# A block's normed, transposed tokens kept in DRAM between two uses; one pool of weight tiles; a new written-out order

## The chip, the cores and the metric

The kernel runs on one core of a Trainium2 chip. TensorE (PE) multiplies matrices, VectorE (DVE) and ScalarE (ACT) work on tiles in SBUF and PSUM, GpSimd (POOL) does a few small operations and issues transfers, and SyncE (SP) only issues transfers. Sixteen DMA engines move the data. The metric is the device time of one execution in microseconds (us), as a median over runs; less is better.

## The reference

Input are 2048 tokens of 512 elements (bf16), eight memory tokens, and the weights of one attention layer (32 heads of 128) and of one gated FFN (512 to 1792 and back). Both layers are applied twice, with the same weights:

```python
x = x + A(layernorm(x), mem0, Wq, Wk, Wv, Wo, 32)
x = x + B(layernorm(x), w_gate, w_up, w_down)
x = x + A(layernorm(x), mem0, Wq, Wk, Wv, Wo, 32)
x = x + B(layernorm(x), w_gate, w_up, w_down)

def A(x, mem0, Wq, Wk, Wv, Wo, seg):      # recurrent over 64 segments of 32 tokens
    mem = mem0
    for s in range(64):
        h = concat(mem, x[32*s : 32*s+32])          # 8 + 32 = 40 tokens
        q, k, v = h @ Wq, h @ Wk, h @ Wv            # per head
        p = softmax(mask(q @ k.T / sqrt(128)))      # memory seen by all, the rest causal
        o = (p @ v) @ Wo
        mem = o[:8]; out[s] = o[8:]
    return concat(out)

def B(x, w_gate, w_up, w_down):
    return (sigmoid(x @ w_gate) * (x @ w_up)) @ w_down
```

The memory makes the segments a chain: a segment's eight memory tokens come from the one before.

## The kernel before

**Steps.** The two passes (job 0 and job 1) run at the same time, job 1 six segments behind job 0 (`lag=6`). Step t handles segment t of job 0 and segment t - 6 of job 1, so there are 70 steps; steps 0 to 5 hold job 0 alone, steps 64 to 69 job 1 alone. A step (`emit_step`, L771 and on) has, for six heads at a time: Q and K projections (L868), scores (L904), mask, maximum, exponential and sum on DVE and ACT, a transpose of the probabilities (L950), the product with V (L976) and the output projection (L995), whose first rows become the next step's memory. The tokens of a step lie transposed in one of eight tiles `hT`.

**Blocks.** Four segments make a block of 128 tokens, sixteen blocks per job. After the last step of a block its FFN runs (`ffn`): transposes back (L1065), residual, LayerNorm, gate and up products (L1097), tanh form of the sigmoid, the down product (L1120). In job 0 the result is normed again and becomes job 1's tokens.

**V.** Most rows of V do not depend on the memory, so V is computed for whole blocks ahead of the steps (`v_pass`, L635, with 128 columns of tokens at a time), written to a DRAM scratch `scr` and read back into `vsb` by the steps. The remaining rows are computed in each step (`strips`, L762). For job 0, ten blocks (2, 14, 3, 4, 5, 7, 8, 10, 11, 13) get their V in `v_group` while the weights are loaded; for 6, 9, 12, 15 and the rest of 14 `v_fill` norms the block and its V rows are done eight at a time, beside job 1's V of some block. Blocks 0 and 1 are taken from `pre1`.

**LayerNorm.** `layernorm_T` (L575 to L596) does statistics on DVE (L582 to L584), a power of -1/2 on POOL (L585), the scaling on DVE into one of two tiles `xn` (L586), and four 128x128 transposes on PE (L595) into a PSUM bank. It is called through `ln_x` for the V of job 0, and again for the same block in `pre1`, which loads the block's tokens into one of six tiles `xs` (L739), norms and transposes them, and copies them into the four `hT` tiles of its segments (`write_hT_x`, L605).

**Weights.** Wq, Wk, Wv, Wo (16.8 MB) stay in SBUF, loaded at the start by SP (L511), each piece of Wv after the piece two before it. The FFN weights do not fit: each block streams them anew, seven pieces each of gate, up and down (256 KB a piece), by POOL (L1089, L1090, L1114) into rings `wg`, `wu`, `wd` of three tiles each. While the weights load at the start these nine tiles serve as staging for V (`bootp`), and every V write of that time carries the key "boot", on which the first loads into the rings wait.

**What sets the order.** All work is first collected as tasks with keys that are read and written. A planner holds an order found elsewhere, stored as a compressed string (`SEQUENCE`), and a bit for each task that may run on either of two engines. `replay` walks through it, gives out buffers of the pools (a free one, or the one freed longest ago), and adds the waits. Instructions are emitted in that order, so each engine and each DMA queue works through its part strictly in sequence. Two further rules: a large weight transfer on POOL waits for a matmul near its planned start (`pace`), and where the plan has PE idle for some time, `warm` puts dummy matmuls on a tile of zeros (L1214). The eight PSUM banks are one pool in which the kinds "bg" and "v" may each hold three at most.

## Time and profile before

| | |
|---|---|
| median of 3 runs (lowest to highest) | 1747.63 us (1746.31 to 1748.25) |
| span of the profiled execution | 1747.1 us; the page gives no other time of it |
| TensorE clock granted, mean | 1.000 |
| PE busy | 1733.4 us |
| DVE, ACT, POOL busy | 1248.4, 1128.5, 859.0 us |
| DMA | 273.41 MB, mean 156 GB/s |

How to read the lines below. PE is a matmul, PEld a weight load into the array, POOLq and SPq the issuing of transfers. The lines of stages give for a stretch its length, the busy time and number of instructions of each engine in the order PE, PEld, DVE, ACT, POOL, then the clock granted to TensorE, the mean busy share of the DMA engines (as transfers overlap it can pass 1) and GB/s. The chain is followed back from the last instruction, at each step to what released it. A group's line has the line number, engine, operation, output and inputs with shapes, the number of instructions; then busy time, the mean duration of one in ns, and the idle time before them with what ended it. Matmuls overlap in the array, so a matmul's duration is longer than the distance from one to the next. L numbers are those of the kernel before.

### The profile page before, as it was taken

What the parts mean: (1) busy time and instruction counts of PE and PEld (TensorE: products, weight loads), DVE (VectorE), ACT (ScalarE), POOL (GpSimd) and SP (SyncE); (2) the same over time, 40 slices, a digit from 0 to 9 for tenths busy, and PEclk for the clock granted to TensorE, in tenths of its full rate; (3) what the DMA queues carried; (4) which work ended last, traced back from release to release, by engine and by line L of the source; (5) the groups of instructions that cost most, each with busy time, mean ns of one, the idle gap of its engine ahead of it and who ended that gap; (6) DMA issues with size and microseconds to landing.
All of it is one profiled execution on the core that took longest, in us unless ns stands there. A gap on an engine that the chain in (4) does not pass through costs nothing.

```text
span 1747.1 us, 91842 instructions
## 1 busy us (share of the span) xinstructions
PE 1733.4 (99%) x39162; PEld 1491.8 (85%) x39162; DVE 1248.4 (71%) x4208; ACT 1128.5 (65%) x3119; POOL 859.0 (49%) x1367
## 2 busy tenths in 40 slices
PE   9999999999999999999999999999999999999998
PEld 4688789889898988989888888989888888988886
DVE  5677777677767776786777767776777776767676
ACT  3576777566666766666666666666665666666564
POOL 5624345635544554445445554544455364454543
PEclk9999999999999999999999999999999999999999
DMA  8935355645645555545555464545455464554644
GB/s 285 320 100 155 109 151 161 195 113 153 174 130 163 156 159 143 165 125 164 152 148 158 136 184 128 166 138 153 132 174 166 139 174 128 144 156 131 178 120 134
DMA packets 145583, 273.41 MB, mean 156 GB/s; under 512 B 39686, under 2 KB 86018, under 8 KB 145174
## 3 DMA queue, kind: packets, MB, share of 16 engines
q0 software_dynamic: 72944, 198.79, 39.8%
q1 hardware_dynamic: 72230, 68.75, 13.3%
q8 instruction: 307, 5.03, 1.2%
q14 instruction: 102, 0.84, 0.2%
HBM read 221.78 MB, written 27.07 MB: 142 GB/s over the span
## 4 chain that ended last, share of the span: by engine, by line
PE 94%; DMA 3%; DVE 1%; SPq 1%; issue 1%; POOL 0%; ACT 0%; POOLq 0%; ACTq 0%
PE bank L868 34%; PE bank L995 17%; PE bank L1097 12%; PE bank L762 8%; PE bank L635 6%; PE bank L1120 6%; PE bank L904 4%; PE bank L976 4%; PE bank L950 2%; PE bank L595 1%; PE bank L1214 1%; DMA wk_sb<-in_A_Wk_dram 1%; DMA wo_sb<-in_A_Wo_dram 0%; PE bank L1065 0%; DMA scr<-wu 0%
## 5 line engine op out<-in xcount | busy, mean ns | idle before, releaser
L868 PE MATMUL bank<-hT,wq_sb 128*128 128x80 bf16 (+3 forms) x8960 | 616.4, 198 | 1.0 <-DVE hT L1008 0.3
L868 PE MATMUL bank<-hT,wk_sb 128*128 128x80 bf16 (+3 forms) x8960 | 616.3, 198 | 0.8 <-DMA wk_sb<-in_A_Wk_dram 0.6
L1228 ACT CAST qku<-bank 128x480 bf16<-128x480 f32 (+4 forms) x770 | 384.7, 508 | 223.7 <-PE bank L868 194.6
L868 PEld LDWEIGHTS <-wq_sb 128*128 128x128 bf16 x8960 | 454.2, 99 | 32.1 <-issue 15.1
L868 PEld LDWEIGHTS <-wk_sb 128*128 128x128 bf16 x8960 | 446.9, 99 | 1.1 <-DMA wk_sb<-in_A_Wk_dram 0.7
L995 PE MATMUL bank<-otsb,wo_sb 128*128 128x80 bf16 (+1 forms) x8960 | 360.2, 198 | 2.2 <-DMA wo_sb<-in_A_Wo_dram 1.3
L918 DVE TENSOR_TENSOR st<-bank,cst 40x240 f32<-40x240 f32 (+3 forms) x768 | 280.5, 368 | 113.2 <-PE bank L904 97.5
L995 PEld LDWEIGHTS <-wo_sb 128*128 128x128 bf16 x8960 | 336.6, 99 | 15.5 <-DMA wo_sb<-in_A_Wo_dram 2.0
L1228 ACT CAST otsb<-bank 128x480 bf16<-128x480 f32 (+3 forms) x420 | 200.2, 483 | 83.4 <-PE bank L976 52.8
L1090 POOL DMA_DIRECT2D wu<-in_B_w_up_dram x217 | 166.5, 768 | 170.0 <-PE bank L950 36.4
L1114 POOL DMA_DIRECT2D wd<-in_B_w_down_dram x217 | 156.9, 723 | 182.0 <-PE bank L1120 39.6
L1224 POOL DMA_DIRECT2D vsb<-sst x351 | 178.2, 512 | 129.6 <-ACT sst L1228 64.7
L1089 POOL DMA_DIRECT2D wg<-in_B_w_gate_dram x217 | 166.4, 767 | 138.1 <-PE bank L1097 56.7
L928 ACT ACTIVATE st<-st 80x240 f32<-80x240 f32 (+3 forms) x420 | 159.2, 381 | 58.0 <-DVE st L925 54.8
L1097 PE MATMUL bank<-xnT,wg 128*128 128x128 bf16 (+2 forms) x1784 | 171.5, 218 | 0.0
L1097 PE MATMUL bank<-xnT,wu 128*128 128x128 bf16 (+2 forms) x1784 | 171.1, 218 | 0.0
L930 DVE TENSOR_REDUCE small<-st 80x6 f32<-80x240 f32 (+3 forms) x420 | 151.5, 363 | 23.4 <-ACT st L928 20.2
L1220 ACT ACTIVATE ptsb<-bank,small 120x160 bf16<-120x160 bf16 (+3 forms) x430 | 156.6, 386 | 17.2 <-PE bank L950 10.7
L904 PE MATMUL bank<-qku 128*128 128x80 bf16 (+1 forms) x2240 | 162.7, 197 | 1.0 <-issue 0.9
L925 DVE TENSOR_TENSOR st<-st,small 80x240 f32<-80x240 f32 (+3 forms) x420 | 155.0, 370 | 5.7
L939 DVE TENSOR_TENSOR pb<-st,small 80x240 bf16<-80x240 f32 (+3 forms) x420 | 154.1, 370 | 5.7
L923 DVE TENSOR_REDUCE small<-st 80x6 f32<-80x240 f32 (+3 forms) x420 | 152.5, 364 | 6.2
(108 smaller groups left out, 2554.1 us busy)
## 6 DMA issues: line engine op xcount, KB each, us to landing
wg<-in_B_w_gate_dram POOLq DMA_DIRECT2D x220, 256.0 KB, 4.2
wu<-in_B_w_up_dram POOLq DMA_DIRECT2D x220, 256.0 KB, 4.2
wd<-in_B_w_down_dram POOLq DMA_DIRECT2D x220, 256.0 KB, 3.9
vsb<-scr SPq DMA_DIRECT2D x137, 66.0 KB
scr<-vst SPq DMA_DIRECT2D x90, 96.0 KB
vsb<-scr POOLq DMA_DIRECT2D x93, 66.0 KB, 3.4
vsb<-sst SPq DMA_DIRECT2D x179, 32.0 KB
vsb<-sst POOLq DMA_DIRECT2D x169, 32.0 KB, 2.8
```

The source lines that it names most:

```text
L868: nc.tensor.matmul(o_ap, lhsT=W[:, c, h * P:(h + 1) * P], rhs=mv(c), start=(c == 0), stop=(c == DC - 1))
L904: nc.tensor.matmul(s_all(SB)[:, w0 + i, :], lhsT=fview(qku[:, i, 0, 0:1], [(1, P)]), rhs=qku[:, i, 1, 0:ncol], start=True, stop=True)
L918: pl.add("DVE", dve_ns(n, True), lambda gsz=gsz, hs=hs, st=st, SB=SB, pj_=pj_, npj_=npj_, mk=mk, idx=idx: nc.vector.tensor_tensor(out=st[p ...
L928: pl.add("ACT", act_ns(n), lambda hs=hs, st=st: nc.scalar.activation(out=st[pr, hs], in_=st[pr, hs], func=ACTF.Exp, scale=self.scale), r=s ...
L995: nc.tensor.matmul(WB[:, c * ncol:(c + 1) * ncol], lhsT=self.wo[:, h, c * P:(c + 1) * P], rhs=otsb[:, hl, 0:ncol], start=(h == 0 and c == ...
L1089: pl.add("POOL", 760, lambda wg=wg, fs=fs: nc.gpsimd.dma_start(out=wg[:], in_=self.wgv[:, :, fs]), r=[("wo", self.H - 1)], w=[gk] + bt, la ...
L1090: pl.add("POOL", 760, lambda wu=wu, fs=fs: nc.gpsimd.dma_start(out=wu[:], in_=self.wuv[:, :, fs]), r=[("wo", self.H - 1)], w=[uk] + bt, la ...
L1097: nc.tensor.matmul(gu[:, 2 * i + k, 0:n], lhsT=W[:, c, i * P:(i + 1) * P], rhs=xnT[:, c, rw], start=(c == 0), stop=(c == DC - 1))
L1114: pl.add("POOL", 760, lambda wd=wd, ip=ip: nc.gpsimd.dma_start(out=wd[:], in_=self.wdv[:, 2 * ip:2 * ip + 2, :]), w=[dk] + (["boot"] if se ...
L1220: nc.scalar.activation(out=dst, in_=src, func=ACTF.Copy, scale=by)
L1224: {"SP": nc.sync, "POOL": nc.gpsimd}[tk.on].dma_start(out=got[1], in_=got[2])
L1228: nc.scalar.copy(out=dst, in_=src)
```

## The change

1. `ln_x` norms and transposes a block once. The result is copied from PSUM into a tile of `vst`, and written to a DRAM tensor `xt` (128 KB per block). The block is noted as kept.
2. A later `ln_x` or `pre1` of a kept block calls `kept_x`: it reads the block from `xt` into one of the two tiles `xn` by SP, and the copies into `hT` are made from there. `pre1` still loads the block's tokens into `xs`, which the residual needs.
3. The three rings of three tiles become one pool `wtp` of nine tiles. A load takes a tile from it, whichever of gate, up and down it is for. V's staging at the start draws on the same pool, and the key "boot" is gone.
4. The pool of PSUM banks has no caps by kind.
5. `SEQUENCE` is a new order, for the new list of tasks.

```diff
+        self.xt = dr.tile([self.NBLK * P, D], BF16, name="xt")
...
-        self.NG, self.ND = 3, 3
-        self.wg = [c.tile([P, DC, 2 * P], BF16, name=f"wg{i}") for i in range(self.NG)]
-        self.wu = [c.tile([P, DC, 2 * P], BF16, name=f"wu{i}") for i in range(self.NG)]
-        self.wd = [c.tile([P, 2, D], BF16, name=f"wd{i}") for i in range(self.ND)]
+        self.wt = [c.tile([P, 1024], BF16, name=f"wt{i}") for i in range(9)]
...
-        self.bank = Pool([...], {"bg": 3, "v": 3}, psum=True)
+        self.bank = Pool([...], psum=True)
...
-        self.bootp = Pool([fview(w[:, 0, 0:1], [(1, 1024)]) for w in self.wd + self.wg + self.wu])
+        self.wtp = Pool(self.wt)
...
     def ln_x(self, b, boot=True):
+        if b in self.kept:
+            return self.kept_x(b)
...
-        return self.layernorm_T(xb[:, :], key)
+        pst, B = self.layernorm_T(xb[:, :], key)
+        nc, pl, D = self.nc, self.pl, self.D
+        tt = pl.buf(self.vstp)
+        pl.add(("ACT", "DVE"), copy_ns(D, True), lambda: (tt[:, 0:D].rearrange("p (c n) -> p c n", c=self.DC), pst()), r=[B], w=[tt])
+        pl.add(("SP", "POOL"), {"SP": 430, "POOL": 590}, lambda: ("dma", self.xt[b * P:(b + 1) * P, :], tt[:, 0:D]), r=[tt], w=[("xt", b)], lat=3000.0, nb=P * D * 2)
+        self.kept.add(b)
+        return pst, B
+
+    def kept_x(self, b):
+        nc, pl, D = self.nc, self.pl, self.D
+        tt = pl.buf(self.xnp)
+        pl.add("SP", 430, lambda: nc.sync.dma_start(out=tt[:, :], in_=self.xt[b * P:(b + 1) * P, :]), r=[("xt", b)], w=[tt], lat=3500.0, nb=P * D * 2)
+        return (lambda: tt[:, :].rearrange("p (c n) -> p c n", c=self.DC)), tt
...
-        pst, B = self.layernorm_T(xb[:], ("xs", i))
+        pst, B = self.kept_x(b) if b in self.kept else self.layernorm_T(xb[:], ("xs", i))
...
+    def weight(self, wt, nm, jp, keys, after):
+        nc = self.nc
+        src = self.wdv[:, 2 * jp:2 * jp + 2, :] if nm == "wd" else (self.wgv if nm == "wg" else self.wuv)[:, :, jp * 2 * P:(jp + 1) * 2 * P]
+        n = 2 if nm == "wd" else self.DC
+        self.pl.add("POOL", 760, lambda: nc.gpsimd.dma_start(out=wt[:, 0:1024].rearrange("p (c f) -> p c f", c=n), in_=src), w=keys, lat=4700.0, nb=370000, r=after)
...
-                gi = self.nxt("wg", self.NG)
-                wg, wu, gk, uk = self.wg[gi], self.wu[gi], ("wg", gi), ("wu", gi)
...
+                wg, wu = gk, uk = pl.buf(self.wtp), pl.buf(self.wtp)
+                for wt, nm in ((wg, "wg"), (wu, "wu")):
+                    self.weight(wt, nm, jp, [wt], [("wo", self.H - 1)])
...
-                di = self.nxt("wd", self.ND)
...
+                wd = dk = pl.buf(self.wtp)
+                self.weight(wd, "wd", ip, [wd], [("wo", self.H - 1)])
```

In the changed kernel the lines move: transposes of LayerNorm are L587, V passes L627, strips L769, Q and K L875, scores L911, output projection L1002, gate and up L1104, down L1125, dummies L1219.

## The prediction

> **What bounds the kernel now.** I read the page first, then busy time by stage, the chain that ended last, and the groups of instructions. From the page:

> ```profile
> span 1747.1 us, 91842 instructions
> PE 1733.4 (99%) x39162; PEld 1491.8 (85%) x39162; DVE 1248.4 (71%) x4208; ACT 1128.5 (65%) x3119; POOL 859.0 (49%) x1367
> ```

> TensorE is idle for 13.7 us of 1747.1. By stage (length, busy time per engine, granted clock, DMA share, GB/s):

> ```profile
> 0.00:10.23 10.23, 9.17 (x36) 3.72 (x37) 4.22 (x13) 1.76 (x2) 3.65 (x19) 1.00 0.70 214
> 10.23:43.68 33.45, 31.09 (x201) 14.41 (x202) 19.64 (x54) 13.75 (x30) 20.85 (x43) 1.00 0.92 306
> 43.68:79.00 35.32, 33.23 (x576) 21.20 (x572) 21.43 (x67) 18.81 (x58) 21.74 (x43) 1.00 1.01 343
> 131.00:1700.00 1569.00, 1566.06 (x35729) 1375.30 (x35727) 1136.13 (x3836) 1032.20 (x2807) 774.45 (x1203) 1.00 0.53 151
> 1700.00:1747.10 47.10, 41.88 (x1089) 33.61 (x1085) 30.39 (x106) 22.33 (x79) 19.12 (x28) 1.00 0.47 134
> ```

> There are two regimes. From 131 to 1700 us TensorE is idle for 2.94 us of 1569, and the DMA engines are half used: only fewer matmuls, or fewer of those few waits, shorten it. The first 79 us look as busy, but from 10 us on the DMA share is 0.92 and then 1.01. The chain says which of the two decides there (start, us, what):

> ```profile
> 18.17 7.47 DMA wv_sb<-in_A_Wv_dram
> 32.51 5.86 DMA wq_sb<-in_A_Wq_dram
> 38.38 7.48 DMA scr<-wu
> 51.15 10.87 DMA wk_sb<-in_A_Wk_dram
> 69.99 8.54 DMA wo_sb<-in_A_Wo_dram
> 78.58 0.84 PE bank L995 x20
> 79.75 2.51 PE bank L868 x96
> ```

> Step 0 ends with matmuls on `wo` (L995) that wait for the last piece of Wo, landed at 78.5 us; step 1 starts at 79.75. Until then the V passes of ten blocks fill TensorE. The load is bound by bytes, the rest by the stream of matmuls.

> **1. Fifteen LayerNorms go.** Before, a block is normed once for V (ten in `v_group`, five in `v_fill`) and all sixteen again in `pre1`: 31. After, blocks 0 and 1 are normed in `pre1` and 2 to 15 once, for V: 16. The written-out order agrees: 60 transposes on L595 fewer. What one takes:

> ```profile
> 12.83 0.61 PE L595 MATMUL bank<-cst,xn 128*128 128x128 bf16 x8
> L595 PE MATMUL bank<-cst,xn 128*128 128x128 bf16 x312 | 29.7, 219 | 0.1
> ```

> Eight take 0.61 us, 0.219 of it the last one's own length: (0.61 - 0.219) / 7 = 56 ns from one to the next, and sixty are 3.4 us. They lie in the stream after the load, where nothing hides a matmul: **-3.4 us**, the one certain term. The other engines' parts, and the nearest rows for the new copy:

> ```profile
> L582 DVE BATCH_NORM_STATS2 small<-xs 128x6 f32<-128x512 bf16 x36 | 24.7, 685 | 5.1 <-DMA xs<-in_A_x_dram 4.8
> L586 DVE TENSOR_SCALAR xn<-xs,small 128x512 bf16<-128x512 bf16 x36 | 15.1, 421 | 4.4 <-POOL small L585 4.1
> L585 POOL TENSOR_TENSOR small<-small,cst 128x1 f32<-128x1 f32 x78 | 46.2, 593 | 154.8 <-DVE small L584 148.4 <-DVE hT L1230 6.1
> L1228 ACT COPY xvf<-bank 128x384 bf16<-128x384 bf16 x4 | 1.9, 474 | 9.5 <-PE bank L595 9.5
> L1228 ACT CAST sst<-bank 128x512 bf16<-128x512 f32 x98 | 57.1, 589 | 63.8 <-PE bank L762 56.1 <-DVE xn L586 3.5 <-PE bank L673 1.5
> ```

> VectorE loses at least 15 x (0.685 + 0.421) = 16.6 us, GpSimd 15 x 0.593 = 8.9. Fourteen copies of 512 elements out of PSUM are new, 0.474 to 0.589 us each, some 7.5 us over two engines that are busy 71% and 65%. I count neither: both hide under TensorE. Where that cover is gone a late copy costs its 0.6 us.

> **2. Fourteen writes of `xt`, fifteen reads, one x load fewer.** Each moves 131 KB. In the body they are 3 MB at a DMA share of 0.53: hidden. In the load they are not. In plan order 24.5 MB stand ahead of the last weight, 23.45 before: V's scratch writes ahead of it are the same 4.89 MB, eight `xt` writes are new (three on SP, five on POOL). At 343 GB/s, the rate of the full stage, their 1.05 MB put the last piece of Wo 3.1 us later. Two things pay back. One more V group, four matmuls on L635, stands before step 1:

> ```profile
> 10.23 2.76 PE L635 MATMUL bank<-wv_sb,xvf 128*128 128x512 bf16 x12
> L635 PE MATMUL bank<-wv_sb,xvf 128*128 128x512 bf16 x224 | 53.2, 379 | 2.4 <-DMA wv_sb<-in_A_Wv_dram 2.4
> ```

> That is 4 x (2.76 - 0.379) / 11 = 0.9 us that later steps need not do. And the stage from 10.23 to 43.68 has 8% of its DMA time free, 2.7 us. With none of it used the load costs 3.1 - 0.9 = +2.2, with all of it -0.5. The chain runs through DMA and the SP queue in that stage too, so its free time is mostly a queue waiting for a copy; I credit 0.8 us of it: **+1.4 us**. [...]

> **3. Queues.** SP goes from 1098 transfers to 1060, GpSimd from 1255 to 1321: 49 loads of V from scratch move from SP to GpSimd, which also takes seven `xt` writes.

> ```profile
> L1224 POOL DMA_DIRECT2D vsb<-scr x176 | 94.8, 540 | 62.3 <-PE bank L976 27.7 <-DMA scr<-vst 14.7 <-PE bank L950 12.1
> L1089 POOL DMA_DIRECT2D wg<-in_B_w_gate_dram x217 | 166.4, 767 | 138.1 <-PE bank L1097 56.7 <-PE bank L995 17.2 <-PE bank L904 13.3
> DMA to landing us min/median/max: 3.2/4.2/6.3
> PE bank L976 <- DMA wg<-in_B_w_gate_dram: 0.2, 1, 0.2
> ```

> 66 x 0.54 - 8.9 = 27 us more on an engine busy for 859 of 1747: covered, unless a weight load stands behind it (below). A read of `xt` waits on SP for one of two `xn` tiles; what stands behind it are V loads and scratch writes, of which more than before go by GpSimd. It then keeps the tile until four copies into `hT` are done, so an FFN's LayerNorm may find one tile only. I count 0; at most five such meetings of one GpSimd step, 5 x 0.593 = 3 us.

> **4. One pool of nine weight tiles, new order, no caps on PSUM kinds.** No instruction is added. Adding up the matmuls in the two orders, step 12 begins after 289 us of work in both, step 57 after 1,443 and 1,440: the removed transposes and no larger move. The new order can at best take away the 2.9 us of waits in the body, and may as well double them: 0, from -2.9 to +2.9. The last 47 us idle for 5.2; the chain of step 69 and the last FFN is the same: 0, within 1.

> **Sum.** 1747.1 - 3.4 + 1.4 = 1745.1 us of span. The page gives no time of that execution beside its span; the median of the runs, 1747.63, is 0.5 above it, so 1745.6 us. No change within 0.2%, 3.5 us, can be told apart.

> **Rivals.** (a) *The load does not grow.* For it: 8% free DMA time, and x rows that now stand first on SP. Against: the chain is DMA up to 78.5 us. Time: 1745.6 - 1.4 - 0.9 (the V group still done early) = 1743.3. With the body's waits gone too it would be 1740.4.

> (b) *A weight load comes late, and the kernel is slower.* With one pool a tile is loaded into whichever was freed longest ago. I took for each of the 672 loads the matmul work between what allows it (the last reader of its tile, or the matmul that paces it) and its first use: under 7.0 us for 28 of them, where before for 4. At the median a load needs 0.77 + 4.2 = 5.0 us, at the worst 0.77 + 6.3 = 7.07. If every tight load took the worst, TensorE would wait 13.4 us in all, before 2.7: +10.7, 1756.3. It decides from 5.4 us on (1745.6 to 1751.0), half of that worst case. Against: all loads have over 5.9 us, and before the worst lateness that TensorE met on a weight queue is 0.2 us, once.

> (c) *TensorE starves in the load, and its clock falls.* The changed order places 14 dummy matmuls inside the load, before step 1, where the old one has none: its plan expects TensorE to run out of V work there. What a cold array costs is seen at the start:

> ```profile
> 1.06 7.77 PE L1214 MATMUL bank<-hot 128*128 128x512 bf16 x23 [1.06 <-DVE cst L484]
> ```

> Those 23 dummies would take 23 x 0.216 = 5.0 us at the spacing of L635, so a cold spell costs 2.8 us. [...] With the whole 3.1 us of bytes, no free room and one cold spell: 1747.6 - 3.4 + 2.2 + 2.8 = 1749.2; with two, 1752.0.

> (d) *It does not do what it says* is excluded: the order itself has 60 transposes fewer.

> **Chances.** Forecast (load longer by a part of 3.1 us) 0.46; (a) 0.34; (b) 0.10; (c) 0.10. Faster than 1744.1 is (a) and a part of the forecast in which waits go as well, less the part of (a) that other waits eat: 0.36. Slower than 1751.1 is (b), a third of (c), and a twentieth for a new order that waits more: 0.18. The rest, 0.46, is no change. The range goes from (a) with most of the body's waits gone, 1741.0, to 1750.5, within reach of one cold spell and of half of (b); the forecast's own is 1744 to 1748.

> **What would show it.** Right: 256 L595 transposes; TensorE idle of about 3 us from 131 to 1700; step 1 starting near 82 us instead of 79.75, released by Wo; GB/s over 300 up to there. Wrong: step 1 at 80 us or earlier (then a); waits of L1104 or L1125 on `wt` from the weights' DMA (b); dummies at a spacing of 0.43 us inside the load (c). A sum of body waits far from 3 us would break part 4, which I hold only by the two orders' likeness.

## The result, and the profile after

The changed kernel takes 1763.31 us (median of 4 runs, 1762.04 to 1764.7), the kernel before 1747.94 on the same chip: a ratio of 1.0081, with a 95% interval from 1.0062 to 1.0100. Measured again in another session it was 1.0091 (1.0073 to 1.0108). The change makes the kernel some 15 us slower. The forecast, 1745.6 us, was wrong, and the time lies outside its range of 1741.0 to 1750.5.

The first two lines of the page of the changed kernel, then its stages as in the prediction (length, busy time of PE, PEld, DVE, ACT, POOL, granted clock, DMA share, GB/s), with one stage added at 79 us:

```profile
span 1762.9 us, 91455 instructions
...
PE 1723.1 (98%) x38901; PEld 1490.8 (85%) x39101; DVE 1234.2 (70%) x4090; ACT 1151.8 (65%) x3191; POOL 879.2 (50%) x1418
```

```profile
10.23:43.68 33.45, 29.19 (x208) 13.70 (x213) 18.76 (x52) 17.46 (x39) 21.44 (x44) 1.00 0.93 296
43.68:79.00 35.32, 29.83 (x417) 17.32 (x418) 17.09 (x51) 18.98 (x53) 23.82 (x44) 0.97 1.07 374
79.00:87.36 8.36, 8.31 (x147) 5.95 (x146) 1.45 (x6) 2.84 (x9) 7.40 (x15) 0.73 0.85 261
131.00:1700.00 1569.00, 1549.24 (x35282) 1367.92 (x35462) 1119.81 (x3714) 1045.74 (x2863) 779.08 (x1226) 1.00 0.53 151
1700.00:1762.90 62.90, 57.21 (x1583) 47.92 (x1583) 39.96 (x141) 33.79 (x117) 23.83 (x35) 1.00 0.44 126
```

The stage from 43.68 to 79 us has 29.83 us of TensorE work in it, where it had 33.23, and 417 matmuls instead of 576; in the one behind it the granted clock is 0.73. (Some 200 matmul records are missing from this trace, 38,901 against 39,101 weight loads, so a part of the idle time from 131 to 1700 us is only missing records; the waits below are not.) The chain that ended last shows what stood still (start, us, what), and the view of PE's waits what it was waiting for over the whole run (us in total, times, longest):

```profile
63.62 2.16 POOL scr L1229 x4
65.78 7.02 DMA scr<-wt
...
73.09 5.58 DMA vsb<-sst
78.80 0.36 PE bank L983 x3
```

```profile
PE bank L983 <- DMA vsb<-sst: 6.5, 4, 4.7
PE bank L627 <- DMA wv_sb<-in_A_Wv_dram: 2.7, 2, 1.7
PE bank L875 <- issue: 2.4, 3, 1.8
PE bank L983 <- DMA vsb<-scr: 2.3, 2, 2.0
PE bank L983 <- DMA scr<-vst: 1.4, 1, 1.4
```

Three of the five are L983, the product with V: TensorE waits for rows of V that are read into `vsb`. (Where the view names a write of the scratch, `scr<-vst` or `scr<-wt`, that is the transfer which ended last before the matmul; that L983 waits for `vsb` there too is read from its inputs.) The kernel before has no such line among its longest waits; its first two are

```profile
PE bank L635 <- DMA wv_sb<-in_A_Wv_dram: 2.4, 2, 1.9
PE bank L995 <- DMA wo_sb<-in_A_Wo_dram: 1.3, 3, 0.6
```

Wo, which the prediction took for the end of the load, is not among the waits after. Step 0's V rows are: POOL issued three of the four reads of its strip (the two lines are POOL's and SP's) from 70.7 us on, the old kernel all four by 61.2 (first and last issue in us):

```profile
L1229 POOL DMA_DIRECT2D vsb<-sst x3: 496/511/514, 70.7 to 73.1; - x3
L1229 SPq DMA_DIRECT2D vsb<-sst x1: 556/556/556, 60.3 to 60.3; - x1
```

```profile
L1224 POOL DMA_DIRECT2D vsb<-sst x4: 504/510/527, 53.3 to 61.2; - x4
```

Where the 15 us went is read best from the starts of the steps: the start of every 256th weight load of the Q and K products in a trace, in us. The new order moves some work between neighbouring steps, so only steps far apart are compared; two kernels of the experiments stand beside.

```
step      before    after   after     all code,   after, V reads and
                            again     old order   weight loads moved
                           (h2)        (f2)          (h1)
   1        79.5     88.0    89.0        80.9         82.0
   3       113.0    123.0   124.0       114.4        115.0
   7       193.8    205.3   207.1       197.2        197.1
  12       309.5    322.3   323.9       312.8        312.7
  16       410.0    426.7   427.2       413.3        413.2
  40      1017.4   1031.7  1034.3      1020.6       1017.5
  69      1713.1   1729.8  1732.3      1714.9       1716.1
```

After against before: +8.5 us at step 1, +10.0 at step 3, +16.7 at step 16, +14.3 at step 40, +16.7 at step 69; the work that moves makes these figures uncertain by some 2 us. So about half is lost in the load and half in the steps, most of it up to step 16. Named places of this trace can account for nearly all of it. In the load they are the wait of 4.68 us for V and 6.83 us at half the clock behind it, which cost at most 3.4. In steps 2, 6, 10 and 14 they are a standstill of 1.85 us, three waits for V of 1.45, 1.19 and 2.00, and 3.41 us at half the clock behind the last, at most 1.7.

### The profile page after: what moved, and what is told of

The parts are those of the page before. It is cut to its first block, busy times and chain, and to the rows that moved or that the text cites. A ratio compares the mean times of both kernels' runs of the same rounds, so it can differ in the third digit from the quotient of the medians.

```text
span 1762.9 us, 91455 instructions
## 1 busy us (share of the span) xinstructions
PE 1723.1 (98%) x38901; PEld 1490.8 (85%) x39101; DVE 1234.2 (70%) x4090; ACT 1151.8 (65%) x3191; POOL 879.2 (50%) x1418
## 4 chain that ended last, share of the span: by engine, by line
PE 86%; DVE 4%; DMA 4%; issue 2%; ACT 2%; POOL 1%; SPq 0%; DVEq 0%; POOLq 0%; ACTq 0%
PE bank L875 30%; PE bank L1002 16%; PE bank L1104 10%; PE bank L769 7%; PE bank L627 6%; PE bank L1125 4%; PE bank L983 4%; PE bank L911 4%; PE bank L957 2%; DMA wv_sb<-in_A_Wv_dram 1%; DMA vsb<-sst 1%; DVE st L925 1%; PE bank L587 1%; DMA scr<-wt 1%; POOL wt L1035 1%
## 5 line engine op out<-in xcount | busy, mean ns | idle before, releaser
L875 PE MATMUL bank<-hT,wq_sb 128*128 128x80 bf16 (+3 forms) x8960 | 615.2, 198 | 2.2 <-DVE hT L1015 0.6
L875 PE MATMUL bank<-hT,wk_sb 128*128 128x80 bf16 (+3 forms) x8960 | 615.1, 198 | 2.0 <-issue 1.8
L875 PEld LDWEIGHTS <-wq_sb 128*128 128x128 bf16 x8960 | 452.9, 99 | 26.3 <-issue 13.2
L875 PEld LDWEIGHTS <-wk_sb 128*128 128x128 bf16 x8960 | 447.0, 99 | 2.3 <-issue 2.3
L1002 PE MATMUL bank<-otsb,wo_sb 128*128 128x80 bf16 (+1 forms) x8960 | 356.1, 198 | 1.1 <-DVE small L937 0.3
L1002 PEld LDWEIGHTS <-wo_sb 128*128 128x128 bf16 x8960 | 333.8, 99 | 11.5 <-issue 1.1
L1104 PE MATMUL bank<-xnT,wt 128*128 128x128 bf16 (+2 forms) x3568 | 242.6, 219 | 1.1 <-issue 0.9
L1035 POOL DMA_DIRECT2D wt<-in_B_w_gate_dram x220 | 168.6, 767 | 119.0 <-PE bank L1104 30.7
L1035 POOL DMA_DIRECT2D wt<-in_B_w_up_dram x220 | 167.7, 763 | 120.5 <-PE bank L1104 25.6
L1035 POOL DMA_DIRECT2D wt<-in_B_w_down_dram x220 | 158.9, 722 | 134.2 <-PE bank L1104 34.0
L1229 POOL DMA_DIRECT2D vsb<-scr x225 | 118.8, 530 | 184.5 <-PE bank L983 82.8
L1104 PEld LDWEIGHTS <-wt 128*128 128x128 bf16 x3568 | 205.7, 98 | 5.4 <-issue 1.8
L1225 ACT ACTIVATE ptsb<-bank,small 80x160 bf16<-80x160 bf16 (+3 forms) x464 | 169.6, 384 | 24.2 <-PE bank L957 18.9
```

Of the source, the lines that this page charges most:

```text
L875: nc.tensor.matmul(o_ap, lhsT=W[:, c, h * P:(h + 1) * P], rhs=mv(c), start=(c == 0), stop=(c == DC - 1))
L1002: nc.tensor.matmul(WB[:, c * ncol:(c + 1) * ncol], lhsT=self.wo[:, h, c * P:(c + 1) * P], rhs=otsb[:, hl, 0:ncol], start=(h == 0 and c == ...
L1035: self.pl.add("POOL", 760, lambda: nc.gpsimd.dma_start(out=wt[:, 0:1024].rearrange("p (c f) -> p c f", c=n), in_=src), w=keys, lat=4700.0, ...
L1104: nc.tensor.matmul(gu[:, 2 * i + k, 0:n], lhsT=W[:, (2 * c + i) * P:(2 * c + i + 1) * P], rhs=xnT[:, c, rw], start=(c == 0), stop=(c == DC ...
L1225: nc.scalar.activation(out=dst, in_=src, func=ACTF.Copy, scale=by)
L1229: {"SP": nc.sync, "POOL": nc.gpsimd}[tk.on].dma_start(out=got[1], in_=got[2])
```

## The experiments

**The theories.** A: the loss is the new order, which puts reads of V late in their queues; the kept tokens and the pool cost nothing. B: the kept tokens crowd the load. C: the one pool lets weight loads collide with reads of V. To part them, the old order was put onto the new code: the same tasks in the old sequence, with the copy, the write and the read of a kept block where its second LayerNorm stood. Each session ran the kernel before beside the others; ratios are to that.

### The parts of the change in the old order

```diff
 e1_kept_old   kernel before
+  ln_x, kept_x, pre1 of the change; rings wg, wu, wd stay
+  kst: one more tile, for the copies of blocks 6, 9, 12, 15
 e2_pool_old   kernel before
+  wtp of nine tiles, weight(), no caps; no kept tokens
 e3_all_old    kernel after
-  new SEQUENCE
+  old SEQUENCE, with 14 copies on ACT, 14 writes on POOL, 15 reads on SP
+  kst, as in e1
```

> The kernel before with the kept tokens alone: its order of tasks is the old one, with a copy on ACT, a write on POOL and a read on SP put in for each kept block where its norm stood (the four copies of the later fills get a tile of their own); the three rings of weight tiles are the old ones. Theory A (the loss of the change is its new order, which issues the V loads of a step late; the kept tokens themselves cost nothing): step 1 starts within 2 us of the 79.5 us before, PE shows no wait of over 2 us for a V load, time 1743 to 1746 us, that is 60 transposes of 56 ns less. Theory B (the writes of the kept tokens crowd the load's DMA): step 1 starts 4 to 8 us late and the time is 1750 to 1756. Theory C (the one pool of weight tiles): 1743 to 1746, as in A.

> The kernel before with the one pool of nine weight tiles and no caps on the PSUM banks, in the old order; norms and transposes as before. Theory A and B: no change, 1746 to 1750 us. Theory C (nine tiles in one pool make weight loads collide with V loads): 1755 us or more, with PE waiting for V loads in steps 7 to 18.

> Everything the change does in code (kept tokens, one pool, no caps), in the old order. What it differs by from the changed kernel (1763.3 us) is the order alone. Theory A: 1743 to 1747 us, so that the order is worth 16 to 20 us. Theory B: 1750 to 1756. Theory C: 1752 to 1763.

Measured: e1 1758.7 us (ratio 1.0063, 1.0051 to 1.0075), e2 1746.33 (0.9993, 0.9985 to 1.0001), e3 1758.87 (1.0065, 1.0050 to 1.0080). In the old order the pool and the missing caps cost nothing, so C falls as a loss that the pool brings by itself. That e1 and e3 were slow looked like B, but the groups of e1 showed another cause. The first line is e1's, the second that of the kernel before:

```profile
L1227 PE MATMUL bank<-hot 128*128 128x512 bf16 (+3 forms) x119 | 29.6, 385 | 1.1 <-DVE cst L482 1.1
```

```profile
L1214 PE MATMUL bank<-hot 128*128 128x512 bf16 (+3 forms) x58 | 16.5, 410 | 1.1 <-DVE cst L484 1.1
```

The planner's replay puts dummy matmuls on `hot` wherever its own clock sees TensorE idle. For the grafted tasks it saw gaps that the chip did not have, and filled them with 13 us of dummies. These two runs therefore say little on the kept tokens.

### The same with the dummies of the kernel before

```diff
-            fill = self.pl.warm(order)
+            fill = the 16 places and sizes of the kernel before (f3: of the changed kernel)
```

> All the code of the change in the old order once more, but with the dummy matmuls of the kernel before (58) in place of the 119 that the planner's own replay put into the first such kernel, which kept PE busy for 13 us more. Theory A (the order alone costs the time): the 13 us go, 1744 to 1747 us, step 1 near 79 us. Theory B (copies and writes of the kept tokens in the load cost time in any order; the dummies only filled waits that were there anyway): PE waits in the load where the dummies were, step 1 starts near 85 us, 1752 to 1757 us.

Measured: 1747.86 us, ratio 1.0007 (0.9997 to 1.0018). All the code of the change in the old order takes as long as the kernel before; the order alone is worth the 1.0081 less 1.0007, some 13 us, by the second session of the changed kernel some 15. Against the kernel before, the order explains the whole of the loss. That does not make the kept tokens free, as A has it: e2, without them, stands at 0.9993, 2.4 us below f2, so the nothing of f2 is, as far as such small differences go, a small gain and a small loss. Nor does f2 hold all of the change: its copies of blocks 6, 9, 12 and 15 have the tile `kst` for themselves, where the changed kernel takes one of `vst`. None of f2's longest waits is for V, but the load has not stayed free, either:

```profile
PE bank L878 <- DMA wq_sb<-in_A_Wq_dram: 1.9, 1, 1.9
PE bank L1005 <- ACT otsb L1236: 1.6, 1, 1.6
```

### The kept tokens of the load

`f4_late_old` is f2 with only blocks 6, 9, 12 and 15 kept, so that nothing is kept in the load. `g1_write_twice` and `h3_copy_twice` are f2 with the write, or the copy, of the ten blocks of the load done twice.

```diff
 f4  ln_x
+        if b not in (6, 9, 12, 15):
+            return pst, B
 g1  the write of a block kept in the load
+            nc.gpsimd.dma_start(out=self.xt2[b * P:(b + 1) * P, :], in_=tt[:, 0:D])
 h3  the copy of a block kept in the load
+            nc.scalar.copy(out=tt[:, 0:D], in_=pst())
```

> The old order with the one pool, and kept tokens for the four blocks of the later fills alone (6, 9, 12, 15): nothing is written in the load. 16 transposes of 56 ns less, 0.9 us, beside the pool's 1746.3 us. Theory A and B: 1744.5 to 1746.5 us. A theory that keeping a block costs time in the body (a PSUM bank held for its copy, a write on POOL ahead of weight loads): 1747 us or more.

> All the code in the old order (1747.9 us), with each of the ten kept blocks of the load written to DRAM twice, to two places: 1.31 MB more in the load. In that order keeping them put step 1 at 80.9 us, against 76.7 with the pool alone. If it is the bytes (1.31 MB at the 343 GB/s that the load moved is 3.8 us): step 1 near 84.7 us, 1751 to 1752.5 us. Rival (it is the ten copies on ACT of 0.48 us, or a tile that they hold): 1747.5 to 1749 us.

> All the code in the old order (1747.9 us), with ACT's copy of the ten kept blocks of the load done twice: 10 copies of 0.48 us more on ACT, no byte more. With the writes done twice it was 2.6 us slower by the ratios to the kernel before. If the copies cost the time: 1750 to 1753 us and step 1 past 83 us. If it is the writes: 1747 to 1749 us and step 1 near 81 us.

Measured: f4 1746.28 us (0.9998, 0.9989 to 1.0006), g1 1750.24 (1.0022, 1.0012 to 1.0033), h3 1749.94 (1.0025, 1.0016 to 1.0035). Step 1 starts at 77.1 us in f4, 76.7 in e2 without any kept block, 80.9 in f2, 83.1 in g1 and 82.9 in h3. So ten kept blocks put the load back by about 4 us in these traces, one of each kernel; f2's has 3.41 us at half the clock among them, at most 1.7 us of loss, and those of e2 and f4 have none. In time f2 is 1.6 us above f4 and 2.4 above e2, by the ratios. Both halves of the work count: doubling the writes costs 2.6 us by the ratios (the 0.0015 between g1 and f2, as much as its uncertainty), doubling the copies 3.1 (0.0018, a little more than its own); the later step 1 of both traces points the same way. A write doubled is 131 KB more and a place more on POOL's queue; these two were not parted. That one of the two would be nothing, as both expectations had for a rival, did not come. What a copy delays is seen in h3, where TensorE waits 2.65 us for ACT's output copy before the product with Wo, and 1.6 in f2:

```profile
76.45 0.96 PE L1010 MATMUL bank<-otsb,wo_sb 128*128 128x40 bf16 x24 [2.65 <-ACT otsb L1241]
```

### Twice the transposes

The steps behind the load should have been 3.4 us shorter in f2. They are not: f2 is 1.4 us behind the kernel before at steps 1 and 3, 3.4 at step 7 and 3.0 at step 60. Of the 2.1 us between steps 3 and 7, 1.2 are lost at one place, and the cause is a copy of the kept tokens. From f2's timeline:

```profile
133.40 0.58 ACT L1236 COPY kst<-bank 128x512 bf16<-128x512 bf16 x1 [1.00 <-DVE xvl L1238]
133.88 0.36 ACT L1236 CAST qku<-bank 128x240 bf16<-128x240 f32 x1
...
134.30 0.32 PE L914 MATMUL bank<-qku 128*128 128x40 bf16 x6 [1.21 <-ACT qku L1236]
```

ACT stands idle for 1.00 us before the new copy, the copy of Q and K that follows it starts only at 133.88 us, and TensorE waits 1.21 us for that. The same wait stands in f4 (1.14) and g5 (1.20); the kernel before and e2 do not have it. Another 0.96 us at step 5 has no releaser in the profile.

For the transposes themselves, the price of one was measured in the other direction.

```diff
 layernorm_T, for pre1 of blocks 2 to 15
-            for c in range(DC):
+            for c in [c for c in range(DC) for _ in range(2)]:
```

> The kernel before, with each LN transpose of the blocks 2 to 15 that enter the steps done twice into the same place: 56 transposes more, nothing else. If a transpose costs the 56 ns of its issue on the path, as the prediction had it: 3.1 us more, 1750 to 1752 us. Rival (they stand between matmuls of Q and K and the scores that wait for ACT's copy, so that PE would stand still there anyway): 1747 to 1748.5 us.

Measured: 1748.59 us, ratio 1.0013 (1.0003 to 1.0023), 2.3 us more. Laid beside the kernel before, weight load by weight load, from 175 to 1510 us, where both run the same matmuls in the same order apart from the transposes:

```
                                      all code, old order (f2)   transposes twice (g3)
change across the places of the
transposes                                    -2.56 us                 +2.89 us
change at all other matmuls                   +2.15                    +0.02
  of it before transposes of the
  probabilities                               +0.51                    -0.04
  before scores, Q and K, output
  projection, product with V                  +1.18                    +0.03
  before gate, up and down products           +0.44                    +0.01
total                                         -0.41                    +2.91
```

Both expectations were half right. A transpose added costs its 56 ns in full (2.89 us for 52 of them). One taken away gives 46 ns at its place (2.56 us for 56), and 2.15 of the 2.56 us come back as small waits. At 403.4 us in the kernel before, for example, f2 gains 0.22 us and has lost 0.13 of it again by 415.3, at a transpose of probabilities, a product with V and a product of scores. Most of these waits are for the engines that feed TensorE: at 16 places of f2, with 1.7 us together, the matmul or its weight load starts 42 or 43 ns after the end of the DVE or ACT instruction that makes its input (`pb`, `ptsb`, `otsb`). The rest was not traced.

### The load of the new order

Step 0's three late reads were moved ahead on POOL's queue.

```diff
 order of POOL, step 0
+  vsb<-scr, vsb<-sst x3
   scr<-wt x12
-  vsb<-scr, vsb<-sst x3
```

> The changed kernel with one thing moved: POOL issues the three V loads of step 0 from the strips' tile ahead of the some 12 writes of the V groups that it issued before them. Theory A: they are issued near 61 us instead of 70.7 to 73.1, PE's wait of 4.7 us at 74 us goes, and the 3.4 us lost at the halved clock behind it go too: step 1 starts near 80 us and the time is 1755 to 1757 us. Theory B or C: the load is bound by the bytes that it moves, the wait moves to another tile, and the time stays within 2 us of 1763.

> The changed kernel with step 0's three V loads issued earlier, as run before, but with the changed kernel's own 57 dummy matmuls instead of the 70 that the replay had made of them (2.3 us more PE time). If the dummies cost what they take: 1755 to 1756 us, against 1757.9 with them; if they stood in waits: no change, 1757.5 to 1758.5.

Measured: e4 1757.93 us (1.0060, 1.0047 to 1.0073), f3 1759.21 (1.0075, 1.0060 to 1.0089). In e4 POOL issues the reads at 58.0 to 59.0 us, no wait for V is left in the load, the clock stays at 1.00, and step 1 starts at 83.3 us instead of 88.0. That is A's mechanism, with less gain than A expected (step 1 near 80 us, 1755 to 1757); the rival's 1761 to 1765 did not come. f3, with 13 dummies fewer, is not faster, so the dummies cost nothing there: they may have stood in waits, or the clock may have stayed at 1.00 in e4's load by them; which it was is not shown. Three of f3's six runs took 1757 us and three 1761 to 1763; the trace is of one of the latter, and in it the clock falls to half twice, from 25.4 us for 6.8 and from 107.3 for 3.4. The move is worth 3.7 to 5.4 us by e4 and 1 to 3 by f3, the latter not clear of noise. What keeps step 1 from 80 us after it was not looked into.

### The burst of weight loads

In step 2 the pool's nine tiles are all free, and the new order has POOL issue nine weight loads in a row, from 95.9 to 104.0 us in the first trace of the changed kernel (93.4 to 101.6 in f3's); the kernel before issues two between 91 and 104 us. In `f6_spread` seven of them come later, from 109.0 to 138.3 us.

```diff
 order of POOL, step 2 (f3 otherwise)
   wt x2
-  wt x7
 ... steps 3 and 4
+  wt, one every 40 to 60 tasks
```

> The kernel with step 0's V loads earlier, and in it seven of the nine weight loads that the pool lets POOL issue in one go in step 2 (near 92 to 103 us) issued later, through steps 3 and 4. Theory: in that burst the DMA share is over 1.0, PE's own instructions come late, and PE stands still for 1.7 us at 102.9 us in the middle of a row of Q and K matmuls with no semaphore; spread, the standstill goes and the time is 1.5 to 2 us below the kernel without the spread. Rival: the standstill has another cause (a wait that the profile does not show), and the time stays within 0.7 us.

Measured: 1756.69 us, ratio 1.0059 (1.0047 to 1.0071), 2.5 us less than f3 in the same session. The two intervals overlap, and the three faster runs of f3 are within 0.7 us of it, so the times alone decide nothing; the traces show what the spreading does. First f3's stages around that place (columns as above), then the line of PE that resumes there in f3's timeline, then f6's stages:

```profile
98.00:100.00 2.00, 2.00 (x47) 1.45 (x44) 1.75 (x10) 1.59 (x8) 2.00 (x4) 1.00 1.13 343
102.00:104.00 2.00, 2.00 (x66) 1.70 (x62) 0.42 (x3) 0.06 (x1) 1.26 (x3) 1.00 1.09 369
104.00:106.00 2.00, 0.03 (x2) 0.00 (x0) 0.00 (x0) 0.56 (x2) 0.00 (x0) 1.00 0.83 259
```

```profile
106.41 0.24 PE L875 MATMUL bank<-hT,wk_sb 128*128 128x54 bf16 x3 [2.38 <-issue]
```

```profile
97.00:99.00 2.00, 2.00 (x58) 1.73 (x57) 1.43 (x7) 1.58 (x8) 0.50 (x1) 1.00 0.53 163
101.00:103.00 2.00, 2.00 (x86) 2.00 (x83) 0.00 (x0) 0.96 (x3) 0.30 (x1) 1.00 0.16 48
```

With the DMA share at 1.09 from 102 to 104 us, TensorE stands still for 2.38 us in the middle of a row of like matmuls, and the profile shows no semaphore for it ("issue"). Spread, the standstill is gone. That the missing thing is PE's own instructions is the author's inference, which no run shows; it rests on this: in four traces a packet of 16,384 bytes on the queue named "instruction" lands 1.3 to 1.6 us before PE goes on, at 106.76 us (on at 108.1) in the changed kernel, 107.64 (109.0) in its second trace, 105.08 (106.4) in f3 and 101.25 (102.9) in e4. Such packets come every 3 to 8 us there, and nothing in the profile ties one to a matmul.

### The steps

The order has 70 steps, and its parts can be exchanged. In `g4_oldload` the first 548 tasks stand as in the old order and the rest as in the new one, in `g5_newload` the reverse.

```diff
 g4   old arrangement | new arrangement behind task 548
 g5   new arrangement | old arrangement behind task 548
```

> All the code of the change; the first 548 tasks of the new order (the load and step 0, up to step 1) stand in the old order's arrangement, all behind them in the new one. All in the old order took 1747.9 us, all in the new 1763.3. If load and steps lose apart from each other, as the starts of the steps say (step 1 is 7.1 us later, the steps up to 18 some 8 more): 1755 to 1757 us. Rival (the steps' stalls follow from the late load): 1748 to 1750 us.

> The reverse: the first 548 tasks as the new order has them, all behind them in the old order's arrangement. Losses apart: 1754 to 1756 us. Rival (all follows from the load): 1760 us or more.

Measured: g5 1755.52 us (1.0048, 1.0031 to 1.0066), as expected: step 1 starts 3.8 us late in its trace, step 69 4.0 late, so behind the new load the old steps lose 0.2 us there. Its six runs take 1751.0 to 1757.8 us and the trace is of the fastest (its wait for V in step 0 is 1.87 us), so half of the median's loss of some 8 us is not in the trace. g4 took 1762.68 (1.0093, 1.0076 to 1.0111), as long as the whole new order, which neither of its two expectations had. It can't decide between them, because of the seam: step 1 starts at 80.0 us, but TensorE then waits 5.59 us at 89.3 for a copy by ACT, which neither order has. Behind it the trace is 10.6 us late at step 3 and 13.7 at step 69.

The changed kernel once more, to see which waits are the order's own:

```diff
 h2   none
```

> The changed kernel itself, for a second trace of it. Every theory expects 1762 to 1765 us. If its waits are fixed by the order, the same ones return: 4 to 5 us for step 0's V loads near 74 us with a halved clock behind it, some 2 us amid the Q and K matmuls near 106 us, and 1 to 2 us each near 198, 297 and 393 us. If they are chance, others stand in their place.

Measured: 1760.28 us, ratio 1.0091. PE's lines with the waits, of the first trace and of the second:

```profile
78.80 0.36 PE L983 MATMUL bank<-ptsb,vsb 80*128 80x80 bf16 x3 [4.68 <-DMA vsb<-sst]
...
197.98 0.74 PE L983 MATMUL bank<-ptsb,vsb 120*128 120x120 bf16 x11 [1.45 <-DMA scr<-vst]
...
297.05 0.44 PE L983 MATMUL bank<-ptsb,vsb 120*128 120x120 bf16 x4 [1.19 <-DMA vsb<-sst]
...
393.31 0.53 PE L983 MATMUL bank<-ptsb,vsb 120*128 120x120 bf16 x7 [2.00 <-DMA vsb<-scr]
```

```profile
80.21 0.36 PE L983 MATMUL bank<-ptsb,vsb 80*128 80x80 bf16 x3 [5.13 <-DMA scr<-wt]
...
199.72 0.74 PE L983 MATMUL bank<-ptsb,vsb 120*128 120x120 bf16 x11 [1.47 <-DMA scr<-vst]
...
298.64 0.44 PE L983 MATMUL bank<-ptsb,vsb 120*128 120x120 bf16 x4 [1.14 <-DMA vsb<-sst]
...
395.43 0.53 PE L983 MATMUL bank<-ptsb,vsb 120*128 120x120 bf16 x7 [2.51 <-DMA vsb<-scr]
```

The same four matmuls wait, for about as long each time. They belong to steps 0, 6, 10 and 14. So the waits are the order's own, but not all of them come each time: the second trace has two more in the same product, 1.19 us in step 18 and 1.94 in step 26, where the first has 0.60 and none, and its standstill amid the Q and K products is 1.09 us, at 109.0. The clock falls to half behind the wait of step 0 in both, behind that of step 14 in the first only. In step 14 the last reads stand on SP behind a read of `xt`, three more reads and a write:

```profile
385.00 1.27 SPq L1229 DMA_DIRECT2D scr<-vst  x1
386.32 0.56 SPq L1229 DMA_DIRECT2D vsb<-sst  x1
387.00 0.50 SPq L739 DMA_DIRECT2D xn<-xt  x1
387.59 1.17 SPq L1229 DMA_DIRECT2D vsb<-sst  x2
388.86 0.50 SPq L1229 DMA_DIRECT2D vsb<-scr  x1
```

That last read landed 4.3 us after its issue, at 393.2, and PE went on at 393.31. In `h1_v_early` the nine last reads of steps 6, 10, 14, 18 and 26 are moved to POOL, to where it issued the step's other reads.

```diff
 order (f6 otherwise)
   POOL  step 14: vsb<-sst ...
+  POOL  step 14: vsb<-sst 7, vsb<-scr 3
-  SP    step 14: vsb<-sst 7, vsb<-scr 3
...
```

> The changed kernel with step 0's V loads earlier and the nine weight loads spread, as run before (1756.7 us), and nine more V loads, the last ones of steps 6, 10, 14, 18 and 26, moved to an earlier place on POOL's queue. Theory (PE waits for the V loads that are issued last: 1.4, 1.2 and 2.0 us in steps 6, 10 and 14 of the changed kernel, with a halved clock behind the last): 4 us less, 1751 to 1753.5 us, and no wait of over 1 us for a V load from step 6 to step 26. Rival (the same wait turns up at the next V load): 1755.5 to 1757.5 us.

Measured: 1750.23 us, ratio 1.0032 (1.0019 to 1.0045), 0.0027 or 4.7 us below f6. From step 6 to step 26 no wait for V of over 0.65 us is left; the 1.1 us of this line stands in step 3, the rest of it in step 18:

```profile
PE bank L983 <- DMA vsb<-scr: 1.8, 2, 1.1
```

The theory gave 1751 to 1753.5, the rival 1755.5 or more. In f6's own trace it was steps 18 and 26 that waited for V (1.03 and 1.99 us), with the clock at half for 3.41 us behind the latter; h1's trace has no half clock at all. Three groups of moved transfers, and no change to the code, thus take the changed kernel from 1.0081 or 1.0091 to 1.0032. What the remaining 0.0025 to f2 (4 us) is was not settled: in the traces h1 is 1.1 us behind f2 at step 1 and 1.2 at step 69, which is a part of it. No version was found that beats the kernel before: e2 and f4 can't be told from it.

## Why the prediction was wrong

**Part 1, the one certain term, -3.4 us, failed in its last step.** The count was right in substance (the trace has 260 transposes, 60 fewer; the 256 of the prediction was a slip), and so were the 56 ns each for a transpose that is added: g3 measures them. "They lie in the stream after the load, where nothing hides a matmul" is what failed: in f2 the stream keeps 0.41 of 2.56 us. TensorE's 2.94 us of idle time did not say that it alone sets the pace; the copies by ACT and DVE arrive only just in time, so a matmul less turns into a wait. "I count neither: both hide under TensorE" failed with it: one new copy in f2's body held TensorE up for 1.2 us, twice the 0.6 that the prediction gave for a late one. Busy time tells what an engine does, not how far behind it the next engine is.

**Part 2, the load, +1.4 us, had the right bytes and the wrong rest.** In the old order the load of f2 ends 1.4 us later than that of the kernel before and 4 us later than that of e2 and f4, whose loads ran better than that of the kernel before. That 1.4 us is the forecast's figure is luck: in e2's trace the pool and the missing caps put step 1 forward by 2.8 us, which the prediction did not have, and in f2's the kept tokens put it back by 4.2. The 3.1 us for the bytes were of the right size: ten doubled writes cost 2.6, give or take as much. Whether the credit of 0.8 for free DMA time was earned can't be told from that. The copies, which were to hide, were worth as much again: 3.1 us for ten doubled ones. In the new order Wo was not the end of the load at all; step 0's reads of V were, and step 1 came at 88.0 instead of 82.

**Part 3, the queues, 0, is the step that lost most of the time.** "66 x 0.54 - 8.9 = 27 us more on an engine busy for 859 of 1747: covered, unless a weight load stands behind it" is a mean over stages, and it asked only for weight loads on that queue. On SP it named the reads of V behind a read of `xt`, and counted 0. What stood behind were reads of V: in the load behind twelve scratch writes on POOL (4.7 and 5.1 us in the two traces), in steps 6, 10 and 14 late on SP's queue (4.6 and 5.1 us in all). The prediction counted how many transfers change queues; it never looked at where a step's last read stands in its queue against its first use, though both orders were at hand.

**Part 4, the new order, 0 from -2.9 to +2.9, failed with it.** It compared the matmul work ahead of steps 12 and 57 and found no larger move. By that measure the work moved little; the transfers did. The body loses 8 us from step 1 to step 69, outside the bounds. The tail was right: 33.1 us behind the start of step 69, 34.0 before.

**The rivals.** (b) did not come: no wait for a weight tile is among PE's longest ones, although 28 loads were tight. With the new order the pool cost time another way, by a burst in which TensorE stood still for 1.1 to 2.4 us. (c) came in its mechanism, not its cause: TensorE starved at 74 us, and behind the wait of 4.68 us the granted clock was 0.50 for 6.83 us, but by late reads and not by bytes. That starving lowers the clock was the author's estimate, which no row of the kernel before shows: its wait of 1.91 us, to 25.69 us, left the clock at 1.00. Its price, 2.8 us a spell, was fair beside at most 3.4 us lost in 6.8 us at half clock; its 1752.0 left out the wait itself. With an order that no run had tried, a chance of 0.18 for slower was low.

## What to carry to other kernels

When a new order comes with a change, run the new code in the old order first: here that parted code that cost nothing on balance from 13 to 15 us of order, once the automatic dummies were held fixed. Predict an order by the last transfer of each stage, its place in its queue and its landing time against the first use, and not by counts per queue or shares of the span. A saving on the busiest engine counts only as far as the engines that feed it are ahead: 0.41 of 2.56 us here.

## What the runs showed of the hardware

The granted clock is recorded in the traces by stretches, of which some are (start and length in us):

```
changed kernel     1.00 from   4.93 for  71.68    0.50 from  76.61 for 6.83    1.00 from  83.44 for 310.61
                   0.50 from 394.05 for   3.41    1.00 from 397.46 for 1365.33
f2                 1.00 from   3.83 for  54.61    0.50 from  58.45 for 3.41    1.00 from  61.86 for 1686.18
f6                 1.00 from  30.23 for 658.77    0.50 from 689.00 for 3.41    1.00 from 692.41 for 1061.55
```

```
trace                       wait of TensorE, us                   granted clock
changed kernel              4.68, to  78.80, for V in step 0      0.50 for 6.83 us, from 76.61
changed kernel again (h2)   5.13, to  80.21, for V in step 0      0.80 on the mean of 79.00 to 87.36
f3                          2.38, to 106.41, no releaser          0.50 for 3.4 us, from 107.3
changed kernel              2.00, to 393.31, for V in step 14     0.50 for 3.41 us, from 394.05
f3                          3.8, for Wv, landed at 26.83          0.50 for 6.8 us, from 25.4
f6                          1.99, for V, landed at 689.05         0.50 for 3.41 us, from 689.00
f2                          1.9, for Wq, landed at 57.58          0.50 for 3.41 us, from 58.45
changed kernel again (h2)   2.51, to 395.43, for V in step 14     1.00
f3                          2.15, to 390.97, for V in step 14     1.00
e4                          2.1, for V                            1.00
kernel before               1.91, to  25.69, for Wv               1.00
changed kernel              1.85, to 108.09, no releaser          1.00
changed kernel              1.45, to 197.98, for V in step 6      1.00
```

By these rows the length of a wait alone does not tell whether the clock falls. What 3.41 us at 0.50 cost is estimated as half of them at most, 1.7 us. The kernel before shows what the first microseconds cost: its dummies stand 427 ns apart up to 6.2 us and 216 ns from 6.6 us on, and its first stretch at 1.00 starts at 6.54.

TensorE stood still amid its Q and K products without a releaser in the profile: for 1.85 and 1.09 us in the two traces of the changed kernel, 2.38 in f3 and 1.65 in e4. The DMA share in a stretch of 2 us ahead of it was 1.06 (104 to 106 us), 1.03 (104 to 106), 1.09 (102 to 104) and 1.07 (100 to 102). In f6 the shares from 97 to 106 us were 0.04 to 0.53, and the longest wait of that kind at these products in the whole trace was 0.8 us.

Reads of V that POOL issued landed 1.6 to 6.7 us after their issue in the first trace of the changed kernel, 2.9 at the median. The last one of step 0 took 5.6 us at the DMA share of 1.07 in the load, and one that SP issued at 290.9 us, beside six weight loads, 6.0. From issue to landing the reads that POOL issued thus differ by up to 5.1 us.
